# Routing step of a fused attention and mixture-of-experts kernel: four columns of one-hots on ScalarE instead of eight, block one-hots moved behind the first tokens, three zero products fewer

## The chip, the core and the metric

The kernel runs on one NeuronCore of one Trainium2 chip. The metric is device microseconds from the start to the end of one execution; the median of the runs of a kernel is its time. The engines are called by the short names of the profile: PE is TensorE (PEld its weight loads), DVE is VectorE, ACT is ScalarE, POOL is GpSimd, SP is SyncE, whose queue carries most of the transfers from HBM.

## What is computed

Two blocks follow each other. The attention block has a batch of 8, 8 heads, 512 tokens and 32 states per head of 64 numbers: the tokens read the states and the states read the tokens, each with its softmax. Its output is put together as 8 × 544 rows of 512 numbers, 4352 tokens in all. The second block sends each token through one of 8 experts:

```python
xread = softmax(scale * x @ state.T) @ state
sread = softmax(scale * state @ x.T) @ x
x = concatenate([xread, sread], axis=2)            # to (8, 544, 512)
...
logits = x @ w_gate;  local_gate = sigmoid(x @ w_local)
for b in range(B):
    prev_e = -1
    for s in range(S):
        fresh_e = argmax(logits[b, s])
        e = fresh_e if s == 0 or local_gate[b, s] < 0.5 else prev_e
        prev_e = e
        p = softmax(logits[b, s])
        h = maximum(x[b, s] @ w1[e], 0)            # 512 -> 1024
        out[b, s] = p[e] * (h @ w2[e])             # 1024 -> 512
```

So a token's expert is its own best one, or that of the token ahead of it, where its local gate says so.

## The kernel before, in words

The kernel has three stages.

**Attention** works through the batches in an order written out by hand (STEPS, L150) and writes each token's row to `rows` in HBM from the SP queue (L446 for 128 token rows, L405 for state rows). Near its end, steps of the attention and of the routing alternate (`reads()` in `Routing.route`).

**Routing** (`Routing.route`, L533 to L785) sorts the tokens by expert. The 4352 tokens stand as 40 columns (COLS) of up to 128 tokens, one token to a partition. Tokens of an expert are put into slots: blocks of 128 slots in pairs, and smaller tiles of 32 slots; there are 49 such blocks (NBLK). For every token the kernel computes its place in a block (`pos`, L661, 0 to 127) and the number of its block (`blk`, L665). To learn which token sits in which slot, it multiplies one-hot matrices on PE: for each of the 40 columns a 128 × 128 matrix that has a one at each token's place is loaded as weights, and a narrow matrix that holds the token's column and partition in the column of its block is streamed through (`slotted`, L712). The 40 products add up in one PSUM bank.

The places' one-hots are made by two engines. ACT makes those of the first eight columns (`inp0`): eight times Abs(index − place) (L680), and one Relu(1 − that) over all eight (L681). DVE makes those of the other 32 in four comparisons of 128 × 1024 (`inps`, L691), one for each eight columns. The narrow matrices exist in two sizes. `bf` (L684, L686) covers only the first two blocks. `bc` covers all 49 blocks; it is made in two halves of 20 columns, each by a comparison on DVE (`blocks`, L700), a scaled copy on ACT (L702) and a product on DVE (`blocks_by_column`, L707).

`slotted` is called three times. The call at L727 (`few`) uses `bf` and gives only the 256 tokens of the first pair of blocks, in the order of columns 8 to 39 and then 0 to 7, so that ACT's columns come last. `tokens` (L718) turns its result into row numbers on DVE (`two`). After the first `yield`, POOL gathers those rows from HBM with an indirect transfer for each block (`gather_first`, L833). The call at L734 (`who`) uses `bc` and gives the tokens of all blocks (`tok`, and `row` by L742 to L745). The third call (L769, `prob`) sorts the probabilities later on.

`keep(n)` (L538) multiplies `place` by an identity n times; the result is used nowhere. Such zero products stand between the calls to keep PE running: 22 ahead of the first call, 3 between the first and the second (L730), 6 after the second (L735).

Every engine takes its instructions in the order of the program. The driver (L1184 to L1196) issues the loads of the first expert's weights, the gather of the first tokens, then the part of the routing up to the second yield, then `turned(0, (0,))` (L851: PE transposes the first gathered block, L862, and DVE and ACT copy it to `xt`, L863), and then the rest of the routing.

**Experts** (from L788) works through pairs of blocks, 256 tokens of one expert each, with weights that stream through rings of nine buffers (`load`, L869). The first pair is multiplied plainly (`plain`, L1098, products at L1106); the others use seven products instead of eight (`strassen`, L1008, products at L1022; `second_half`, L1051, products at L1062), with sums of weight blocks on DVE (L936). Small tiles of 32 tokens are done between (L910, L922). POOL gathers later tokens quarter by quarter (L827) and scatters results (L1002, L932).

Of the kernel before, what the change touches and what calls it, by code (L numbers as in the profile page):

```python
# [10 lines left out]
BF16 = mybir.dt.bfloat16  # L11
Act = mybir.ActivationFunctionType
Alu = mybir.AluOpType
# [5 lines left out]
P = 128  # L19
# [12 lines left out]
COLS = B * NC  # L32
# [12 lines left out]
CG = 4  # L45
NG = COLS // CG
# [4 lines left out]
def kernel(  # L51
# [43 lines left out]
    with ExitStack() as phase, ExitStack() as late:  # L95
        p = late.enter_context(tc.tile_pool(name="p", bufs=4, space=PSUM, side="right"))
        reads = late.enter_context(tc.tile_pool(name="reads", bufs=1, side="right"))
        lt = reads.tile([P, B, NC, SQ], F32, name="lt")
        with ExitStack() as early:
            make_identity(nc, ident)  # L100
            start = Attention(early, tc, p, reads, xn, xt, st, stt, wgl, wgs, lt, rows, none)
            route.constants(ident)
            start.clear()
            route.more_constants()
            start.run(route)
        bank = Banks(tc, 4)
        routing = route.route(bank, lt, slots, start.reads, rows)
        experts(phase, late, tc, bank, w1, w2, rows, slots, route, routing, out)
# [63 lines left out]
class Attention:  # L172
# [50 lines left out]
    def run(self, route):  # L223

        self.route = route
        self.keep(10)
        self.steps = [(name, [int(i) for i in at]) for name, at in ((s[:2], s[2:]) for s in STEPS.split())]
        self.reads()
# [16 lines left out]
    def bank(self, parts=P, n=512):  # L245
        return self.p.tile([parts, n], F32, tag="p", name="p")
# [202 lines left out]
class Routing:  # L449
# [83 lines left out]
    def route(self, bank, lt, slots, reads, rows):  # L533
        nc, rt, ex = self.nc, self.rt, self.ex
        iof, iob, identb, part, cols, before, ones, one, ev, on, turn, quarter, place = self.consts
        exf = ex.rearrange("p b i -> p (b i)")

        def keep(n):  # L538

            to = bank.sums or [bank()]  # L540
            for i in range(n):
                nc.tensor.matmul(to[i % len(to)], lhsT=identb, rhs=place.rearrange("p k c -> p (k c)"), start=True, stop=True)
# [117 lines left out]
        pos = rt.tile([P, COLS], BF16, name="pos")  # L660
# [8 lines left out]
        def over(x, n=NBLK):  # L669
            return x.rearrange("p (g o c) -> p g o c", o=1, c=CG).to_broadcast([P, x.shape[1] // CG, n, CG])  # L670

        def each(x, n=NG):
            return x.rearrange("p (o k) c -> p o k c", o=1).to_broadcast([P, n, x.shape[1], CG])


        n = 2 * CG
        off = rt.tile([P, n, P], BF16, name="off")
        inp0 = rt.tile([P, n, P], BF16, name="inp0")
        for c in range(n):
# [6 lines left out]
        nc.vector.tensor_tensor(bf.rearrange("p d g k c -> p d (g k c)"),  # L686
                                inf.rearrange("p (o g) k c -> p o (g k c)", o=1).to_broadcast([P, 2, 2 * NG * CG]),
                                self.factors.rearrange("p d g k c -> p d (g k c)"), op=Alu.mult)
        inps = [rt.tile([P, 2, P, CG], BF16, name=f"inp{i}") for i in range(1, NG // 2)]
        for i, inp in enumerate(inps, 1):  # L690
            nc.vector.tensor_tensor(inp, each(place, 2), over(pos[:, i * n:i * n + n], P), op=Alu.is_equal)  # L691

        inb = rt.tile([P, NG, NBLK, CG], BF16, name="inb")
        pb = rt.tile([P, 3, NG, NBLK, CG], BF16, name="pb")
# [3 lines left out]
        def blocks(h):  # L698
            g = halves[h]
            nc.vector.tensor_tensor(inb[:, g], each(place[:, :NBLK], NG // 2),  # L700
                                    over(blk[:, g.start * CG:g.stop * CG]), op=Alu.is_equal)
            nc.scalar.activation(bc[:, 1, g].rearrange("p g k c -> p (g k c)"),  # L702
                                 inb[:, g].rearrange("p g k c -> p (g k c)"), Act.Copy, scale=part)

        def blocks_by_column(h):
            g = halves[h]
            nc.vector.tensor_tensor(bc[:, 0, g], inb[:, g], over(cols[:, g.start * CG:g.stop * CG]), op=Alu.mult)  # L707

        blocks(0)
        blocks_by_column(0)  # L710

        def slotted(to, x, order=(*range(n, COLS), *range(n))):  # L712
            for c in order:
                lhs = inp0[:, c] if c < n else inps[c // n - 1][:, c // CG % 2, :, c % CG]
                nc.tensor.matmul(to, lhsT=lhs, rhs=x[:, :, c // CG, :, c % CG],  # L715
                                 start=(c == order[0]), stop=(c == order[-1]))

        def tokens(to, who):  # L718
            high = rt.tile([P, to.shape[1]], F32, name="high")
            nc.vector.tensor_scalar(high, who[:, 0], -float(LOW), float(NT), Alu.mult, Alu.add)  # L720
            nc.vector.tensor_tensor(to, high, who[:, 1], op=Alu.add)
# [3 lines left out]
                            in_=rows[:NT].rearrange("(b t) q x -> q b t x", b=B)[0:1, :, 0:S + 1:S, 0])  # L725
        few = bank()[:, :4].rearrange("p (d k) -> p d k", d=2)
        slotted(few, bf)  # L727
        tokens(slots.two, few)
        yield
        keep(3)  # L730
        blocks(1)
        blocks_by_column(1)
        who = bank()[:, :2 * NBLK].rearrange("p (d k) -> p d k", d=2)
        slotted(who, bc, range(COLS))  # L734
        keep(6)  # L735
        wd = rt.tile([P, 2, NBLK], BF16, name="wd")
        nc.vector.tensor_copy(wd, who)
        tokens(slots.tok, who)
# [12 lines left out]
        def probabilities():  # L751
# [15 lines left out]
            prob = bank()[:, :3 * NBLK].rearrange("p (d k) -> p d k", d=3)  # L767
            yield
            slotted(prob, pb)  # L769
            nc.vector.tensor_copy(slots.prob, prob[:, 0])  # L770
            for d in (1, 2):
# [473 lines left out]
```

## Time and profile before

| | us |
|---|---|
| median of 3 runs | 546.63 |
| the 3 runs | 543.44, 546.63, 547.95 |
| the profiled execution's own time | 543.85 |
| its span, first to last instruction | 542.1 |
| busy in the span: PE, PEld, DVE, ACT, POOL | 525.3, 459.1, 381.2, 174.6, 314.4 |
| PE's mean granted clock in the span | 0.994 of full speed |

The profile is of one execution, and 1.75 us of its time lie outside the span. The routing stands between about 71 and 96 us of the span, its last part overlapping the start of the experts. The chain of waits follows the work that ended last back to its start; a row gives the start in us, the length in us, and the engine, tile and line. In a timeline a row is start, length, engine, line, operation, tiles and sizes, how many instructions were merged, and in square brackets how long the engine stood idle before it and what released it. In a table by window the columns are the window, its length, the busy time of each engine with its number of instructions, the granted PE clock (1.00 is full speed), the share of the DMA engines' time and the rate in GB/s.

### The profile page before, as it was taken

The numbers are of one execution on the slowest core, as the hardware profiler recorded it, in microseconds if no ns is written. First come the engines' busy times: TensorE is split into PE (matmuls) and PEld (weight loads), VectorE is DVE, ScalarE is ACT, GpSimd is POOL, SyncE is SP. The second block draws the span as 40 slices with busy tenths as digits, with TensorE's granted clock in tenths as the row PEclk, the third lists the DMA queues.
The fourth block names the chain that finished last, engine by engine and source line by source line (L and its number), as shares of the span: only waits on it lengthen the run. The fifth ranks groups of instructions, "written<-read, shape, count | busy, mean of one in ns | idle before, by whom it ended". The sixth has DMA issues, their size and how long they took to land.

```text
span 542.1 us, 12973 instructions
## 1 busy us (share of the span) xinstructions
PE 525.3 (97%) x4923; PEld 459.1 (85%) x4923; DVE 381.2 (70%) x618; ACT 174.6 (32%) x362; POOL 314.4 (58%) x384
## 2 busy tenths in 40 slices
PE   8799989999999999999999999999999999999994
PEld 3567776988989898989898989889999998989994
DVE  6999976656776657575765748386776767777774
ACT  6688754102223222222222222223132222213220
POOL 7788702563675746555555555565757474746653
PEclk9899999999999999999999999999999999999998
DMA  8999867699989899898989898974658484746652
GB/s 322 394 327 371 284 251 235 234 396 392 407 287 386 314 352 352 312 367 288 379 291 358 302 362 298 347 238 158 226 193 281 133 312 125 276 151 240 239 187 100
DMA packets 48970, 155.39 MB, mean 287 GB/s; under 512 B 6849, under 2 KB 8001, under 8 KB 45570
## 3 DMA queue, kind: packets, MB, share of 16 engines
q1 hardware_dynamic: 41234, 135.78, 68.9%
q0 software_dynamic: 7520, 18.62, 9.8%
q8 instruction: 41, 0.67, 0.5%
q14 instruction: 31, 0.25, 0.1%
q10 hardware_dynamic: 144, 0.07, 0.0%
HBM read 136.61 MB, written 17.89 MB: 285 GB/s over the span
## 4 chain that ended last, share of the span: by engine, by line
PE 89%; DVE 4%; DMA 3%; POOL 1%; ACT 1%; issue 1%; ACTq 0%; DVEq 0%
PE ps L1062 23%; PE ps L1022 20%; PE sum L1022 15%; PE sum L1062 13%; PE p L432 3%; PE ps L922 3%; PE ps L910 3%; PE ps L1106 3%; DMA x_n<-in_xn_dram 2%; PE ps L715 2%; PE s L307 1%; PE p L390 1%; DMA x_t<-in_xt_dram 1%; PE p L377 1%; POOL e L367 1%
## 5 line engine op out<-in xcount | busy, mean ns | idle before, releaser
L827 POOL DMA_INDIRECT xg<-rows,row x131 | 157.5, 1203 | 34.5 <-issue 32.9
L936 DVE TENSOR_TENSOR a<-a,a 128x1024 f32<-128x1024 f32 x64 | 76.8, 1220 | 30.5 <-DMA a<-in_w_dram 29.1
L1022 PE MATMUL ps<-xt,a 128*128 128x128 f32 x720 | 88.6, 276 | 0.0
L1022 PE MATMUL sum<-xs,a 128*128 128x128 f32 x720 | 87.8, 275 | 0.0
L1022 PEld LDWEIGHTS ps<-xt,a 128*128 128x128 f32 x720 | 84.4, 192 | 2.1 <-issue 1.8
L1022 PEld LDWEIGHTS sum<-xs,a 128*128 128x128 f32 x720 | 84.0, 192 | 0.0
L936 DVE TENSOR_TENSOR c<-c,c 128x1024 f32<-128x1024 f32 x64 | 75.4, 1219 | 3.8 <-DMA c<-in_w_dram 3.1
L1062 PE MATMUL ps<-c,h 128*128 128x256 f32 x312 | 74.7, 382 | 0.0
L1062 PEld LDWEIGHTS ps<-c,h 128*128 128x128 f32 x312 | 58.0, 190 | 10.9 <-issue 3.7
L1062 PE MATMUL ps<-c,hs 128*128 128x256 f32 x256 | 60.5, 379 | 0.0
L1002 POOL DMA_INDIRECT out_dram<-y,tok x32 | 38.6, 1205 | 28.8 <-DVE y L1089 14.5
L1062 PEld LDWEIGHTS ps<-c,hs 128*128 128x128 f32 x256 | 48.6, 190 | 6.6
L1062 PE MATMUL sum<-c,h 128*128 128x256 f32 x200 | 47.2, 379 | 0.0
L936 DVE TENSOR_TENSOR h<-s,s 128x512 f32<-128x512 f32 x15 | 10.4, 694 | 49.7 <-ACT s L1045 49.7
L1062 PEld LDWEIGHTS sum<-c,h 128*128 128x128 f32 x200 | 38.0, 190 | 5.2
L841 POOL COPY tick<-r 1x1 f32<-1x1 f32 x41 | 16.4, 401 | 42.8 <-ACT r L1067 40.1
L970 ACT COPY sum<-ps 128x256 f32<-128x256 f32 (+1 forms) x31 | 14.3, 460 | 71.1 <-PE ps L1022 49.5
L841 POOL COPY tick<-s 1x1 f32<-1x1 f32 x45 | 14.7, 327 | 36.8 <-ACT s L1045 36.8
L855 DVE STREAM_TRANSPOSE xt<-xg 128x512 f32<-128x512 f32 x32 | 33.5, 1083 | 1.0 <-DMA xg<-rows,row 1.0
L432 PE MATMUL p<-sd,a 128*128 128x256 f32 x128 | 32.1, 390 | 0.2 <-ACT xr L438 0.2
L1067 ACT ACTIVATE r<-sum,prob 128x256 f32<-128x256 f32 x32 | 15.1, 473 | 52.0 <-PE sum L1062 52.0
L1062 PE MATMUL sum<-c,hs 128*128 128x256 f32 x128 | 30.2, 379 | 0.0
(227 smaller groups left out, 756.8 us busy)
## 6 DMA issues: line engine op xcount, KB each, us to landing
a<-in_w_dram SPq DMA_DIRECT2D x68, 512.0 KB, 8.4
c<-in_w_dram SPq DMA_DIRECT2D x68, 512.0 KB, 10.6
at<-in_w_dram SPq DMA_DIRECT2D x18, 1024.0 KB, 10.9
ct<-in_w_dram SPq DMA_DIRECT2D x18, 1024.0 KB
x_t<-in_xt_dram SPq DMA_DIRECT2D x16, 512.0 KB, 7.8
x_n<-in_xn_dram SPq DMA_DIRECT2D x8, 1024.0 KB, 10.9
rows<-xr SPq DMA_DIRECT2D x32, 256.0 KB, 3.0
xg<-rows,row POOLq DMA_INDIRECT x131, 5.2
```

Source lines behind the costliest of these rows:

```text
L432: self.nc.tensor.matmul(v[:, d], lhsT=self.get("a", b, u)[:, c * P:c * P + P], rhs=self.sd[:, b, d], start=True, stop=True)
L827: nc.gpsimd.indirect_dma_start(out=to.rearrange("p x k -> p (x k)"), out_offset=None, in_=rows.rearrange("n q x -> (n q) x"), in_offset=ba ...
L841: nc.gpsimd.tensor_copy(tick, value)
L855: nc.vector.transpose(to.rearrange("p k (i t) -> p k i t", i=Q), xgs_[u % 2][:, b].rearrange("p i x k -> p k i x"))
L910: nc.tensor.matmul(hps[SQ * g:SQ * g + SQ, :], lhsT=self.x_t[:, j, :], rhs=a[:, j, :, g], start=(j == 0), stop=(j == KT - 1))
L922: nc.tensor.matmul(yps[SQ * g:SQ * g + SQ, :], lhsT=self.h[:, m, :], rhs=ct_[:, 2 * m // FK, g // 2, m % (FK // 2), g % 2 * P:g % 2 * P + ...
L936: nc.vector.tensor_tensor(out, a, b, op=op)
L1002: put = nc.gpsimd.indirect_dma_start(out=out, out_offset=to, in_=y, in_offset=None, bounds_check=NT - 1, oob_is_err=False)
L1022: nc.tensor.matmul(to[:, m * P:m * P + P], lhsT=w[:, j, m * P:m * P + P], rhs=x[:, j, :], start=begin and m == 0 and j == 0, stop=(m == FK ...
L1062: nc.tensor.matmul(to, lhsT=x[:, m, :], rhs=w[:, m, :], start=begin and m == 0, stop=(m == FK // 2 - 1), skip_group_check=True)
L1067: nc.scalar.activation(to, t, Act.Copy, scale=p)
L1106: nc.tensor.matmul(hps[:, i * P:i * P + P], lhsT=a[n][j // 2][:, j % 2, i * P:i * P + P], rhs=x_t[:, j, b * P:b * P + P], start=(j == 0), ...
```

## The change

Four things change.

1. ACT makes the one-hots of four columns instead of eight: `n` is now CG, which is 4, so that L680 issues four Abs instead of eight, and L681's Relu covers 128 × 512 instead of 128 × 1024. DVE makes the other 36: one comparison of 128 × 512 for columns 4 to 7, then four of 128 × 1024 for columns 8 to 39.
2. `slotted` takes columns 4 to 31, then ACT's 0 to 3, then 32 to 39, so that the last comparison of DVE comes last.
3. `blocks(0)` and `blocks_by_column(0)` stand behind `tokens(slots.two, few)`, ahead of the yield. On DVE all four operations for the 49 blocks now follow `two` directly; before, two of them stood ahead of it. ACT's two scaled copies follow their comparisons.
4. The second call of `slotted` is followed by three zero products instead of six.

```diff
-        n = 2 * CG
+        n = CG
         off = rt.tile([P, n, P], BF16, name="off")
         inp0 = rt.tile([P, n, P], BF16, name="inp0")
         for c in range(n):
...
-        inps = [rt.tile([P, 2, P, CG], BF16, name=f"inp{i}") for i in range(1, NG // 2)]
-        for i, inp in enumerate(inps, 1):
-            nc.vector.tensor_tensor(inp, each(place, 2), over(pos[:, i * n:i * n + n], P), op=Alu.is_equal)
+        inps = {}
+        for g, k in ((1, 1), *((g, 2) for g in range(2, NG, 2))):
+            inp = rt.tile([P, k, P, CG], BF16, name=f"inp{g}")
+            nc.vector.tensor_tensor(inp, each(place, k), over(pos[:, g * CG:(g + k) * CG], P), op=Alu.is_equal)
+            for i in range(k):
+                inps[g + i] = inp[:, i]
...
-        blocks(0)
-        blocks_by_column(0)
-
-        def slotted(to, x, order=(*range(n, COLS), *range(n))):
+        def slotted(to, x, order=(*range(n, COLS - 2 * CG), *range(n), *range(COLS - 2 * CG, COLS))):
             for c in order:
-                lhs = inp0[:, c] if c < n else inps[c // n - 1][:, c // CG % 2, :, c % CG]
+                lhs = inp0[:, c] if c < n else inps[c // CG][:, :, c % CG]
                 nc.tensor.matmul(to, lhsT=lhs, rhs=x[:, :, c // CG, :, c % CG],
...
         few = bank()[:, :4].rearrange("p (d k) -> p d k", d=2)
         slotted(few, bf)
         tokens(slots.two, few)
+        blocks(0)
+        blocks_by_column(0)
         yield
         keep(3)
         blocks(1)
         blocks_by_column(1)
         who = bank()[:, :2 * NBLK].rearrange("p (d k) -> p d k", d=2)
         slotted(who, bc, range(COLS))
-        keep(6)
+        keep(3)
```

## The prediction

> **What bounds the kernel now.** I began with the page: the span, the busy times, and the chain of work that ended last, by engine and line.
>
> ```profile
> span 542.1 us, 12973 instructions
> PE 525.3 (97%) x4923; PEld 459.1 (85%) x4923; DVE 381.2 (70%) x618; ACT 174.6 (32%) x362; POOL 314.4 (58%) x384
> PE 89%; DVE 4%; DMA 3%; POOL 1%; ACT 1%; issue 1%; ACTq 0%; DVEq 0%
> ```
>
> PE is the bound over the whole span; its products of the experts follow each other from 96.3 us on. A change in the routing therefore counts by one thing: when PE can begin the experts' first product (L1106). I then took the chain in order of time between 84 and 97 us.
>
> ```profile
> 84.77 2.46 ACT off L680 x8
> 87.25 1.07 ACT inp L681
> 88.37 0.35 PE ps L715 x8
> 88.72 0.67 PE sum L542 x3
> 89.39 3.85 PE ps L715 x40
> 93.24 1.30 PE sum L542 x6
> 94.53 0.76 issue
> 95.29 0.49 PE ps L862 x2
> 95.81 0.43 DVE xt L863
> 96.28 0.82 PE ps L1106 x5
> ```
>
> The chain runs through ACT's one-hots and then along PE's queue to the end of the six zero products (94.53). It says "issue" for 0.76 us because it doesn't connect the gather. L862 transposes the first gathered block, so the two paths into it are PE's queue (free at 94.53) and the gather. The timeline by engine shows the second path:
>
> ```profile
> 84.99 2.49 DVE L691 TENSOR_TENSOR inp<-place,pos 128x1024 bf16<-128x1024 bf16 x4
> 88.95 0.16 DVE L721 TENSOR_TENSOR two<-high,ps 128x2 int32<-128x2 f32 x1
> 89.72 0.67 DVE L707 TENSOR_TENSOR pb<-inb,cols 128x980 bf16<-128x980 bf16 x1
> 90.17 1.17 POOL L833 DMA_INDIRECT y<-rows,two  x1 [4.39 <-DMA a<-in_w_dram]
> ```
>
> `two` is done at 89.11, the gather starts 1.06 us later, is issued at 91.34, and L862 starts 3.92 us after that, when its rows have landed. The profile names a load of `a` as what released POOL. In the program the gather waits for `two` and for writes of `rows` and work of the attention done before 86, not for `a`; I take `two` as its releaser. So the gather ends last, 0.76 us behind PE.
>
> **Part 1 and 2: the one-hots.** ACT has four Abs instead of eight: 84.77 + 4 × 2.46/8 = 86.00. Its Relu on 512 instead of 1024 elements costs about 0.68 (from 1.06 for 1024 and 0.39 for an Abs on 128), so ACT ends at 86.70 instead of 88.32, a gain of 1.6 that is no longer the last wait: DVE is next. DVE gets a comparison of 512 elements ahead of its four. From 681 ns for 1024 and 241 ns for L686's 160 elements of bf16 it is 0.42 long; the four started 0.60 apart, 0.08 less than they last, so it adds 0.34. DVE ends at 84.99 + 2.49 + 0.34 = 87.82. PE's last eight products, now on DVE's strided layout, took 0.43 in such a group before, and start 0.06 after DVE: 88.31 instead of 88.72. `two` follows at +0.39: 88.70. Gain on the gather's path: **0.41**.
>
> **Part 3: the blocks behind `two`.** On DVE four operations follow at 88.62 (they overlap the end of `two` by 0.08, as before): two comparisons of 0.66 and two products of 0.67, with the small steps between them that the trace has: `inb` of the first half to 89.28, its product to 89.98, the second half's to 90.61 and 91.31. ACT's scaled copies, about 1.11 each, run 89.31 to 90.43 and 90.64 to 91.76. The second call of `slotted` waits for both results of the first half, so it starts at 90.49 instead of 89.36. Its 20 products of that half (3.85/40 each) end at 92.41, the second half is ready by then, and all end at **94.34** instead of 93.24. This is what the move costs on PE's queue: 1.1. Behind that wait stand the zero products, L862, L742 and all experts' products.
>
> **Part 4: three zero products fewer** give back 1.30/2 = 0.65: PE is free at 94.99 instead of 94.53. That was 0.76 ahead of the rows and is now about level with them; with six it would be 95.64.
>
> **The gather beside DVE.** With `two` at 88.70 the gather would start at 89.76, in the middle of DVE's four operations, where before only the rest of one (to 90.39) ran beside it. Here a rule of the Trainium skill speaks against the change. The page SBUF — State Buffer, section "SBUF: two separate sides", says that VectorE and GpSimd share a port pair under an exclusive lock, held for a whole instruction, and that POOL cannot write a transfer's descriptors while DVE holds it. Read strictly, with DVE's operations back to back, the gather would wait for the last one: 91.31 + 0.95 = 92.26, 0.92 later than now. The trace has this situation:
>
> ```profile
> 106.53 4.79 DVE L936 TENSOR_TENSOR c<-c,c 128x1024 f32<-128x1024 f32 x4 [3.10 <-DMA c<-in_w_dram]
> 107.96 1.94 POOL L827 DMA_INDIRECT xg<-rows,row  x1 [0.16 <-issue]
> 110.39 1.78 POOL L827 DMA_INDIRECT xg<-rows,row  x1 [0.16 <-issue]
> ```
>
> A gather alone takes 0.97. DVE's boundaries in that row are about 1.20 apart: 107.73, 108.93, 110.12, 111.32. The first gather ends at 109.90 and the second at 112.17, both 0.85 to 0.97 after the next boundary, although DVE went on at once in the first case. The one beside `two` fits too: 90.39 + 0.95 = 91.34. So a gather loses the rest of one DVE operation, not the whole burst. I take that: the boundary at 89.98 plus 0.95 is 90.93 instead of 91.34, and 0.41 of gain stays. Landing follows at +3.92: 94.85.
>
> **The sum.** L862 starts when the later of the two has come: PE's queue at 94.99, the rows at 94.85. That is about 95.0 instead of 95.29, a gain of **0.29**. What follows is relative to it: `wd` is ready about 94.7 for L742, the first weights of `a` landed at about 91.5, the loads of `c` wait for L754 on DVE behind it, and PE has no gap up to the end. The third call of `slotted` has the same 40 products in another order and no wait. The queues of SP and POOL keep their order. On the profiled execution it is 543.85 − 0.29 = 543.56; the median of the runs lies 2.78 above that execution, so 546.63 − 0.29 = **546.3**.
>
> **Rivals.**
> *The transfer sets the landing* (no gain). The loads of `a` keep the DMA engines at 0.86 to 1.10 of their time until 91.5. If the gathered rows queue behind them they land when they did, 95.26: change 0, 546.6. Against it: most of the gathers' traffic in the windows comes between 92 and 95, after those loads.
>
> *The port stays with DVE for the burst.* The gather is issued at 92.26, the rows land at 96.18, 0.9 later than now: 547.5. The two rows above speak against it; for it speaks only the page.
>
> *PE's clock drops* (slower). The new order leaves PE idle from the end of the three zero products (88.31 + 0.67 = 88.98) to 90.49, 1.5 us, behind a stretch of products only four columns wide (86.4 to 88.3). The trace has one gap after which the clock fell. Its rows, in order: the chain's first work after the gap, two windows of half a microsecond around the fall (the clock is the number behind POOL's bracket), and from PE's timeline a shorter gap:
>
> ```profile
> 16.81 1.93 PE p L390 x64
> 15.50:16.00 0.50, 0.00 (x0) 0.00 (x0) 0.47 (x2) 0.50 (x2) 0.44 (x1) 1.00 1.21 500
> 16.50:17.00 0.50, 0.19 (x9) 0.22 (x13) 0.50 (x2) 0.50 (x1) 0.50 (x2) 0.50 1.04 434
> 68.40 0.65 PE L422 MATMUL p<-a,gl 128*32 128x128 f32 x16 [1.14 <-DVE rt L400]
> ```
>
> PE stopped at 14.17, the clock still stood at 1.00 at 16.0 and was at half from about 16.3 for 3.4 us; the 64 products of L390 took 1.93 instead of 1.10. After a gap of 1.14 (the last row) it stayed at 1.00. My 1.5 lies between 1.14 and about 2.1, nearer the harmless one. If the clock falls as the second call starts, 3.4 us at 1.75 times the time cost 1.5 on PE's queue, 94.99 becomes 96.4 or 96.5, and the kernel loses 1.2; a drop in the fp32 products behind it costs up to 1.7. That is 547.8 to 548.3. It decides from a gap of some 2 us on, or sooner if the narrow products count as idle.
>
> **How the numbers follow.** Likeliest, gain of 0.1 to 0.5: 0.62, own range 546.1 to 546.5. No gain, because the transfer sets it: 0.17. Clock: 0.12. Port: 0.07. Something that the trace doesn't show: 0.02. No case reaches 1% (5.5 us), which is about what a measurement of this kernel can tell from no change: the three runs shown lie between 0.6% below their median and 0.2% above. So within 1%: 0.96; slower 0.03, since the unpriced risks (clock, port) lie on that side; faster 0.01. The range is made of the cases, −0.5 to +1.7, and of the spread of the runs, which is larger than any of them: 543.6 to 548.3.
>
> **What the next profile would show.** Right: ACT's Relu done at about 86.7 and the last comparison at 87.8; `two` at 88.7; the gather issued by 90.9; the second call from about 90.5 to 94.3; L862 at about 95.0; granted clock 1.00 from 86 to 96. Wrong: L862 at or after 95.3, with the clock below 1 around 90 to 94, or with a gather longer than 1.9 us, or with PE idle ahead of L862 though the gather was issued early. What would move the time by 1% is nothing in these 12 us; it would be a gap in the experts' stage, where PE has none now.

## The result

The change makes no measurable difference: the median after it is 547.08 us and before it 547.13 us, of 22 runs each; the ratio of the runs (not that of the two medians) is 1.0009, with a 95% interval of 0.9995 to 1.0022. The forecast was 546.3, no change that can be told, with a gain of 0.29 inside it. That gain isn't there.

The profiled execution after the change took 546.23 us, its span 544.3. The chain of work in order of time, from DVE's one-hots to the experts' first product (start us, us, what):

```profile
84.55 2.75 DVE inp L692 x5
87.36 0.44 PE ps L715 x8
88.01 0.16 DVE two L721
88.78 1.12 ACT pb L705
89.95 3.88 PE ps L715 x40
93.83 1.01 PE sum L542 x3
94.83 0.44 PE ps L864 x2
95.30 0.44 DVE xt L865
95.78 1.27 PE ps L1108 x9
```

The clock time of this stage moves by a microsecond from one execution to the next, since the attention ahead of it doesn't always take as long. I count from the end of `pos` (L661 ended at 84.48 before and at 83.95 here), to which the one-hots are tied. L864 after the change is L862 of before, and L1108 is L1106.

| from the end of `pos`, us | before | predicted | after |
|---|---|---|---|
| DVE's last comparison done | 3.00 | 3.34 | 3.35 |
| first call of `slotted` done | 4.24 | 3.83 | 3.85 |
| `two` done | 4.63 | 4.22 | 4.22 |
| gather starts | 5.69 | 5.28 | 5.28 |
| gather issued | 6.86 | 6.45 | 6.45 |
| second call starts | 4.91 | 6.01 | 6.00 |
| second call done | 8.76 | 9.86 | 9.88 |
| zero products done | 10.05 | 10.51 | 10.89 |
| first transposes of `y` start | 10.81 | 10.5 | 10.88 |
| experts' first product starts | 11.80 | 11.5 | 11.83 |

Down to the second call each step lies within 0.02 us of the forecast. Then two things go wrong: the zero products take longer, and the rows don't come earlier. The windows show the first: the columns are PE, PEld, DVE, ACT and POOL with their busy time, then the granted clock, the DMA share and the rate.

```profile
88.50:89.00 0.50, 0.00 (x0) 0.00 (x0) 0.47 (x2) 0.21 (x1) 0.00 (x0) 1.00 1.12 393
90.50:91.00 0.50, 0.50 (x8) 0.50 (x7) 0.24 (x1) 0.50 (x1) 0.30 (x1) 1.00 0.80 328
91.00:91.50 0.50, 0.50 (x9) 0.50 (x6) 0.00 (x0) 0.18 (x1) 0.50 (x1) 0.51 1.13 303
93.50:94.00 0.50, 0.50 (x5) 0.27 (x3) 0.07 (x1) 0.00 (x0) 0.00 (x0) 0.50 0.23 90
94.50:95.00 0.50, 0.50 (x4) 0.25 (x3) 0.05 (x1) 0.00 (x0) 0.00 (x0) 1.00 0.04 16
```

PE's clock falls to half at about 91.0 and is back at 94.4. The second call runs through it in 3.88 us, as long as at the full clock (3.85), but three zero products take 1.01 instead of 0.65. The second is in the timelines of POOL and of PE's weight loads:

```profile
89.23 1.17 POOL L835 DMA_INDIRECT y<-rows,two  x1 [4.07 <-DMA a<-in_w_dram]
94.75 0.56 PEld L864 LDWEIGHTS ps<-ident,y 128*128 128x128 f32 x4 [0.55 <-issue]
```

The gather starts 0.41 sooner than before, counted from `pos`, but the weight load of the first transpose starts only at 94.75, which is 4.35 after the gather was issued instead of 3.92. So the rows came at 10.80, about level with the end of the zero products. The experiments take the two apart.

### The profile page after: what moved, and what is told of

Same layout as the page of the kernel before. It is cut to its first block, busy times and chain, and to the rows that moved or that the text cites. A ratio compares the mean times of both kernels' runs of the same rounds, so it can differ in the third digit from the quotient of the medians.

```text
span 544.3 us, 12961 instructions
## 1 busy us (share of the span) xinstructions
PE 526.4 (97%) x4917; PEld 459.4 (84%) x4920; DVE 381.0 (70%) x619; ACT 173.0 (32%) x358; POOL 317.7 (58%) x384
## 4 chain that ended last, share of the span: by engine, by line
PE 88%; DVE 6%; DMA 3%; POOL 1%; issue 1%; ACT 0%; ACTq 0%; DVEq 0%
PE ps L1064 23%; PE ps L1024 20%; PE sum L1024 15%; PE sum L1064 13%; PE ps L924 3%; PE ps L912 3%; PE p L432 3%; PE ps L1108 3%; DMA x_n<-in_xn_dram 2%; PE ps L715 2%; DVE a L371 1%; DMA x_t<-in_xt_dram 1%; PE p L390 1%; PE p L377 1%; DVE e L334 1%
## 5 line engine op out<-in xcount | busy, mean ns | idle before, releaser
L1064 PEld LDWEIGHTS ps<-c,h 128*128 128x128 f32 x312 | 58.0, 190 | 10.9 <-issue 3.7
L843 POOL COPY tick<-r 1x1 f32<-1x1 f32 x41 | 19.2, 467 | 42.4 <-ACT r L1069 39.7
L843 POOL COPY tick<-s 1x1 f32<-1x1 f32 x45 | 16.4, 364 | 43.6 <-ACT s L1047 43.4
```

The lines of the kernel that those rows point to most:

```text
L843: nc.gpsimd.tensor_copy(tick, value)
L1064: nc.tensor.matmul(to, lhsT=x[:, m, :], rhs=w[:, m, :], start=begin and m == 0, stop=(m == FK // 2 - 1), skip_group_check=True)
```

## The experiments

Lines named in an expectation are those of its own kernel; one inserted or removed line shifts them by one. The variants with the gap filled, with none behind (both), with all of `a` held back and with each large part alone ran once each; one time says little here, so I go by their profiles.

**The gap filled.** Nine zero products instead of three between the first and the second call.

```diff
         yield
-        keep(3)
+        keep(9)
         blocks(1)
```

> The changed kernel with nine zero products instead of three behind the first call of slotted, which fill the 1.5 us in which PE stood idle there. Times are counted from the end of pos (L661); in the changed kernel the second call runs from 5.99 to 9.87, the zero products behind it to 10.87, and L864 starts there (before the change: 10.81). Theory (the clock fell in that idle gap, and its whole price is the zero products behind the second call): clock 1.00 throughout, the second call still takes 3.9, the three zero products behind it 0.67 instead of 1.01, and L864 starts at 10.5 to 10.55. Rival (the clock falls because of the stretch of narrow products, not of the gap): clock at half again, L864 at 10.85. Rival (the rows hold L864): zero products done at 10.5, L864 still at 10.8. The total time shows none of this: within 0.3 us of the changed kernel, under the spread of the runs.

The chain (`pos` ends at 84.10) and PE's weight load in its timeline:

```profile
90.10 3.88 PE ps L715 x40
93.98 0.65 PE sum L542 x3
94.63 0.22 issue
94.86 0.49 PE ps L864 x2
```

```profile
94.82 0.56 PEld L864 LDWEIGHTS ps<-ident,y 128*128 128x128 f32 x4 [0.69 <-issue]
```

The clock stays at 1.00 and the zero products take 0.65: with the idle gap filled, the clock doesn't fall. The other profiles agree: in all six kernels here with nine zero products in that place the clock is at 1.00 throughout the second call, and in all four profiles with a gap of 1.50 it falls during the call. But the transposes start at 10.76, not at 10.5: PE stands idle for 0.22, and the rows hold it. Theory and second rival are both right in part: the clock's price was 0.36, and behind it stood a second wait of nearly the same end.

**No zero products behind the second call**, once with three and once with nine ahead of it.

```diff
         slotted(who, bc, range(COLS))
-        keep(3)
         wd = rt.tile([P, 2, NBLK], BF16, name="wd")
```

> The changed kernel without any zero products behind the second call. This shows when the gathered rows have landed. Theory (PE's queue sets L864, the rows land about 10.0 from the end of pos, since the DMA engines are quiet from there on): L864 at 10.0 to 10.1, 0.8 earlier than in the changed kernel. Rival (the rows land 3.92 after the gather is issued, as the prediction took it): L864 at 10.37. If the clock is still at half there, the four transposes of L864 take longer than 0.72.

> The changed kernel with nine zero products behind the first call (the clock stays up) and none behind the second. PE is then free for L863 at 9.88 from the end of pos. In the kernels so far the first rows landed 10.8 to 11.1 after SP began to issue the loads of a, whether the gather started 5.4 or 6.5 after that. Theory (the landing is set by the loads of a, behind which the rows' packets drain; the rival the transfer sets the landing): L863 at 10.7 to 10.9, so PE stands idle for about 0.9 and nothing is gained. Rival (the rows land 3.92 after the gather is issued): 10.37.

With three ahead (`pos` ends at 84.76), PE waits 1.15 us for the rows and L863 starts at 11.02, so the theory of an early landing at 10.0 falls and so does 10.37. With nine ahead (`pos` ends at 83.65), L863 starts at 10.37. That is the rival's number to the digit, and alone it would have misled me. Counted from SP's issue of the loads of `a` instead, the two are 11.1 and 10.8, and every kernel falls into place. The rows' landing is read from the start of the first transpose's weight load, behind its idle time. The rows for it, of before and of the one-hots alone, whose gather starts latest:

```profile
84.38 1.95 SPq L879 DMA_DIRECT2D a<-in_w_dram  x4
95.26 0.56 PEld L862 LDWEIGHTS ps<-ident,y 128*128 128x128 f32 x4 [1.22 <-issue]
```

```profile
83.86 1.95 SPq L882 DMA_DIRECT2D a<-in_w_dram  x4
90.13 1.17 POOL L836 DMA_INDIRECT y<-rows,two  x1 [4.88 <-DMA a<-in_w_dram]
94.77 0.56 PEld L865 LDWEIGHTS ps<-ident,y 128*128 128x128 f32 x4 [0.77 <-issue]
```

| from the start of `a`'s issue on SP, us | gather starts | gather issued | rows landed |
|---|---|---|---|
| before | 5.79 | 6.96 | 10.88 |
| after | 5.46 | 6.63 | 10.98 |
| after, on another chip | 5.40 | 6.57 | 10.78 |
| gap filled | 5.45 | 6.62 | 10.89 |
| three ahead, none behind | 5.40 | 6.57 | 11.11 |
| nine ahead, none behind | 5.75 | 6.92 | 10.81 |
| one-hots alone (below) | 6.27 | 7.44 | 10.91 |

The gather moves by 0.87 us; the landing stays within 0.33 and doesn't follow it. (In the two profiles of the changed kernel PE's products leave no gap, and it is the weight load ahead of them that stands idle. In the second it starts 0.30 before its product, so it may have waited for PE; there 10.78 is only the latest that the rows can have come.) `two` can come earlier or later in this range, and the rows land at a fixed time from the issue of `a`'s loads.

Without zero products PE's queue can also pay in another way: with nine ahead and none behind, a gap of 0.49 is followed by a fall of the clock at 94.2, as the transposes run, and the first 32 of the experts' products take 4.78 instead of 3.84 (chain of work).

```profile
94.02 1.02 PE ps L863 x4
95.37 4.78 PE ps L1107 x32
```

**The loads of `a` taken out of the way.** Nine zero products ahead and none behind as above, and the loads wait for DVE's copy of the expert's number behind `row`:

```diff
-        e = index(slots.experts[0:1, u - 1:u] if u else slots.again if i else slots.expert)
+        e = index(slots.experts[0:1, u - 1:u] if u else slots.again)
...
-    load(0, 0)
     gather_first()
...
+    load(0, 0)
     load(0, 1)
```

> As the kernel with nine zero products behind the first call and none behind the second, but the loads of a (2 MB) are not issued ahead of the gather: they wait for the copy of the expert's number that DVE makes behind row, as the loads of c do. This takes away the traffic that the gather's rows are said to drain behind, and costs the experts' first product its early weights. Theory (a's loads set the landing): the rows land about 3.5 after the gather starts, at 8.8 to 9.2 from the end of pos, and L863 starts at once behind the second call, at 9.9; the experts' first product then waits for a until about 16.5, so the run is some 4 to 5 us longer. Rival (a fixed time from issue to landing): L863 at 10.4 or later.

POOL's gather and its landing in the view of the tile `y` (`pos` ends at 85.33):

```profile
90.60 1.17 POOL L834 DMA_INDIRECT y<-rows,two  x1 [4.45 <-DVE inb L703]
```

```profile
DMA to landing us min/median/max: 3.4/3.4/3.4
```

The same view of the kernel that differs only in the loads (nine ahead, none behind):

```profile
DMA to landing us min/median/max: 5.0/5.0/5.0
```

PE's transposes and the experts' first product with the loads held back:

```profile
95.02 0.66 PE L863 MATMUL ps<-ident,y 128*128 128x128 f32 x4
102.52 5.69 PE L1107 MATMUL ps<-xt,a 128*128 128x128 f32 x23 [6.57 <-DMA a<-in_w_dram]
```

Without the 2 MB of `a` the rows land 3.4 us after the gather starts, at 8.7, and not 5.0 to 5.6 as in those profiles with `a`'s loads ahead that give it (gap filled 5.4, three ahead 5.6, nine ahead 5.0, the changed kernel on another chip 5.3); the transposes follow the second call without a gap, at 9.7. So it is the loads of `a` that put the landing off. How they hold the rows isn't shown. Summed over windows of a quarter of a microsecond, 1.9 of the 2.1 MB of `a` had been moved when the gather of before was issued; from there to the landing it was 0.75 MB, of which 0.52 are the two gathers' rows. So most of `a` had been moved, and yet the rows came late. The experts' first product waits for its weights, as expected, to 17.2. The time is 553.23 in the one run, 9.4 above before; I expected 4 to 5, and 5.4 of it lie ahead of the first product. Its first products also run at half clock after the gap, and the stretch from there to PE's end is 3.3 longer; where the rest lies stays open.

**Half of `a` held back.** As the last, but two quarters are loaded early and two wait for a copy of the expert's number made right behind `wd`.

```diff
         nc.vector.tensor_copy(wd, who)
+        nc.vector.tensor_copy(slots.again, slots.expert)
...
-            nc.vector.tensor_copy(slots.again, slots.expert)
             nc.vector.tensor_copy(slots.experts, others)
...
-        e = index(slots.experts[0:1, u - 1:u] if u else slots.again if i else slots.expert)
+        e = index(slots.experts[0:1, u - 1:u] if u else slots.again if i or quarters.start else slots.expert)
...
-    load(0, 0)
+    load(0, 0, slice(2))
     gather_first()
     next(routing)
+    load(0, 0, slice(2, 4))
     turned(0, (0,))
```

> As the kernel with nine zero products behind the first call and none behind the second, but only the first two quarters of a (1 MB) are issued ahead of the gather; the other two wait for a copy of the expert's number that DVE makes right behind wd, and so run in the stretch from 95 to 98 us in which the DMA engines stood idle. Theory (a's loads set the landing): the rows land by 9.9 from the end of pos, L863 starts at 9.9 to 10.0 and the experts' first product at 10.9 instead of 11.8; the later quarters land at about 15, just when they are needed. Gain 0.9 us, ratio 0.9984. Rival (the landing has another cause): L863 at 10.4 to 10.8, and the time as before or longer, if the late quarters are waited for.

```profile
94.76 0.66 PE L863 MATMUL ps<-ident,y 128*128 128x128 f32 x4
96.38 0.82 PE L1107 MATMUL ps<-xt,a 128*128 128x128 f32 x5 [0.69 <-DVE xt L864]
```

The rows land 3.5 after the gather starts, and the transposes follow the second call without a gap, at 9.7 from the end of `pos` (85.04). But the first product starts at 11.34, not 10.9. It waits for a new last: the copy to `xt` stands on DVE behind `wd`, `again`, `high` and `tok`, and all four are due just then. The ratio is 0.9996, with an interval of 0.9982 to 1.0011.

**The same with that wait removed**: the copy of the number goes behind `blocks_by_column(1)`, and ACT makes both copies to `xt`.

```diff
         blocks(1)
         blocks_by_column(1)
+        nc.vector.tensor_copy(slots.again, slots.expert)
...
         nc.vector.tensor_copy(wd, who)
-        nc.vector.tensor_copy(slots.again, slots.expert)
...
-            for h, copy in enumerate((nc.scalar.copy if b else nc.vector.tensor_copy, nc.scalar.copy)):
+            for h, copy in enumerate((nc.scalar.copy, nc.scalar.copy)):
```

> As the kernel that holds half of a back, with two more edits. The copy of the expert's number is made right behind the last block operation on DVE, so that the late quarters of a are issued about 2.5 us sooner, behind the gather's packets. And both halves of the first xt are copied by ACT, so that the first copy no longer waits for DVE's wd, high and tok. Theory (with the rows landed early, PE's queue up to the end of the second call is the bound): L863 at 9.9 from the end of pos as in that kernel, the experts' first product at 10.6 to 10.7 instead of 11.3 there and 11.8 before the change; gain against before the change 1.1 to 1.2 us, ratio 0.9979. Rival (the sooner quarters of a delay the rows again): L863 at 10.4 or later, and no gain.

The timeline of PE (`pos` ends at 83.89):

```profile
89.90 3.87 PE L715 MATMUL ps<-pb,inp 128*128 128x98 bf16 x40 [0.20 <-ACT pb L705]
93.59 0.66 PE L863 MATMUL ps<-ident,y 128*128 128x128 f32 x4
94.89 3.81 PE L1107 MATMUL ps<-xt,a 128*128 128x128 f32 x32 [0.37 <-ACT xt L864]
```

The first product starts at 11.00, 0.80 earlier than before the change; I expected 10.6 to 10.7, and the last row has PE waiting 0.37 for ACT's copies. The median is 542.73 against 543.60 of before on that chip, the ratio 0.9989 with an interval of 0.9971 to 1.0008. In the profile this version beats both kernels; in the time it can't be told from them.

**Each large part alone.** First the new one-hots with the blocks where they were and six zero products (the diff is against the changed kernel); then the move of the blocks with the one-hots and the six zero products of before (against the kernel before).

```diff
+        blocks(0)
+        blocks_by_column(0)
+
         def slotted(to, x, order=(*range(n, COLS - 2 * CG), *range(n), *range(COLS - 2 * CG, COLS))):
...
         tokens(slots.two, few)
-        blocks(0)
-        blocks_by_column(0)
         yield
...
         slotted(who, bc, range(COLS))
-        keep(3)
+        keep(6)
```

> The change of the one-hots alone: four columns on ACT, the others on DVE in the new order, but the blocks' one-hots where they were before the change and six zero products. Theory (DVE's queue decides: the two block operations now stand between DVE's last comparison and the reading of the first call's result): few done at 3.84 from the end of pos, two only at about 5.05 instead of 4.63 before the change and 4.21 after it, the gather starts at 6.1, and L862 starts at about 11.2, 0.4 later than before the change. Rival (only ACT's end mattered): two at 4.2 and L862 at 10.4.

```diff
-        blocks(0)
-        blocks_by_column(0)
-
         def slotted(to, x, order=(*range(n, COLS), *range(n))):
...
         tokens(slots.two, few)
+        blocks(0)
+        blocks_by_column(0)
         yield
```

> The move of the blocks' one-hots alone: one-hots of eight columns on ACT as before the change, six zero products, the blocks behind two. Theory (two hangs on ACT's one-hots, done 3.84 after the end of pos, and not on the blocks): two at 4.6 as before the change, the gather issued at about 6.85, the second call starts 0.4 later than in the changed kernel, at 6.4, and ends at 10.3; PE stands idle 1.5 us again and the clock falls, so that the six zero products take about 2.0 to 2.3 instead of 1.30, and L862 starts at 12.3 to 12.6, 1.5 to 1.8 later than before the change. Rival (the clock does not fall): 11.6.

With the one-hots alone (`pos` ends at 84.17) `two` is done at 4.90 and the gather starts at 5.96, 0.27 later than before the change, which is DVE's queue as the theory says, though less of it. Yet L865 starts at 10.63, sooner than before and not 0.4 later, since the rows land with the loads of `a`, which were issued 0.31 before the end of `pos` here and 0.10 before the change. The clock fell in this kernel too (windows as above):

```profile
88.50:89.00 0.50, 0.17 (x1) 0.00 (x0) 0.47 (x4) 0.50 (x1) 0.00 (x0) 1.00 1.08 377
89.00:89.50 0.50, 0.20 (x3) 0.30 (x4) 0.50 (x2) 0.25 (x1) 0.00 (x0) 0.58 0.84 279
```

It fell at 89.1, inside a gap of 0.63 ahead of the second call, and was back at 92.5. The second call, most of it at half clock, took 3.89, and the six zero products behind it ran at full clock and took 1.30, so this fall cost nothing.

With the move alone (`pos` ends at 85.43) the second call runs from 6.41 to 10.29, as expected, the clock falls during it, and six zero products take 1.62 instead of the 2.0 to 2.3 that I gave them. The transposes start at 11.75 to 11.9, and the first product at 12.65, 0.85 later than before the change. Its first gather began 6.47 after `a`'s issue, later than any in the table, and in the view of `y` landed 4.4 after its start: at 10.9 from `a`'s issue once more, although the windows have 2.1 MB moved by the time it was issued. So the move by itself costs 0.85 on PE's queue; the sooner one-hots and the dropped zero products only pay that back.

**Does a delay here count one for one?** Nine zero products ahead and 33 behind the second call (`keep(9)`, `keep(33)`).

> The changed kernel with nine zero products behind the first call and 33 behind the second. The 30 more than in the changed kernel are 6.5 us of PE time ahead of L864. Theory (everything behind L864 is relative to it, so that a delay there counts one for one): L864 at 17.0 from the end of pos instead of 10.8, and the time 6.2 longer than before the change, ratio 1.0113. Rival (the experts' stage has slack of its own, for instance the loads of weights, so that a shift is partly taken up): 2 to 4 us longer.

The chain (`pos` ends at 85.16):

```profile
102.16 0.24 PE ps L864 x2
102.90 0.38 PE ps L1108
```

L864 starts at 17.0 and the first product at 17.74, 5.94 later than before; from there to the end of PE's last product it is 438.8, as before. So in the profile the delay counts one for one, and there is no slack. In the time it is more than that: the ratio is 1.0151, interval 1.0128 to 1.0174, thus at least 6.9 us where I expected 6.2. The theory's number is missed, and the profile of one execution doesn't show where the rest lies; it stays open.

**The changed kernel once more**, on another chip.

> The changed kernel once more, on another chip, beside the kernel before. In its first profile the stretch from the experts' first product to the end of PE's work took 441.8 us, in the profiles of before and of four variants 438.8. Theory (those 2.9 us belong to that execution and not to the change): 438.8 here, the experts' first product again at 11.8 to 11.9 from the end of pos, ratio 1.000. Rival (the change costs the experts' stage something, say by the place of its buffers): 441 to 442 again and a ratio of 1.003 to 1.005.

In the first profile after the change, the stretch from the first product (95.78) to the end of PE's last was 441.8, in that of before 438.8. The last product in that first profile, and in this one (chain of work):

```profile
535.80 1.74 PE ps L1064 x8
```

```profile
93.85 1.28 PE sum L542 x3
95.13 0.24 PE ps L864 x2
95.87 2.16 PE ps L1108 x17
532.97 1.74 PE ps L1064 x8
```

Here it is 534.71 − 95.87 = 438.84, and the ratio is 0.9997, interval 0.9984 to 1.0010. The 2.9 us belonged to that execution: they lie in many small stretches between pairs, such as 2.06 to 2.27 instead of 1.88 for the 64 products of L924, and this second profile of the same kernel has none of them (1.88 to 1.89). The clock fell here too, at 91.6, and the three zero products took 1.28. The first product starts at 11.89.

## Why the prediction was right, and where it was wrong

The verdict, no change that can be told, and the range held, and they would have held with either sign of the 0.29: the median of before itself is 0.50 higher over 22 runs than over the three of the forecast. That they held says nothing for the gain, and the account of the gain didn't hold.

*The one-hots and the blocks* (parts 1 to 3) were right in every term to 0.02. ACT stopped being the last wait, DVE took its place, and `two` gained 0.41. The second call was pushed back by 1.1.

*The gather beside DVE.* The gather came when I said, and the rival of the port rested on too wide a reading of the page SBUF — State Buffer. Its section "SBUF: two separate sides" says that POOL can't write descriptors while DVE runs an operation in a 2-port mode; a DVE operation with two SBUF inputs, as these four have, takes the lock only against a POOL operation that reads SBUF, as the gather reads `two`, and for that instruction. The trace of before agrees: beside L936, with two such inputs, a gather took 1.44, beside a transpose, with one input, 0.97:

```profile
126.39 2.51 DVE L936 TENSOR_TENSOR a<-a,a 128x1024 f32<-128x1024 f32 x2 [6.83 <-DMA a<-in_w_dram]
127.04 1.44 POOL L827 DMA_INDIRECT xg<-rows,row  x1 [0.48 <-issue]
128.81 2.09 DVE L855 STREAM_TRANSPOSE xt<-xg 128x512 f32<-128x512 f32 x2
129.10 0.97 POOL L827 DMA_INDIRECT xg<-rows,row  x1 [0.16 <-issue]
```

DVE after the change:

```profile
88.78 0.67 DVE L710 TENSOR_TENSOR pb<-inb,cols 128x980 bf16<-128x980 bf16 x1
89.37 0.66 DVE L703 TENSOR_TENSOR inb<-place,blk 128x980 bf16<-128x980 bf16 x1
90.07 0.67 DVE L710 TENSOR_TENSOR pb<-inb,cols 128x980 bf16<-128x980 bf16 x1
```

The gather started at 89.23; the operation running then ended at 89.45; 89.45 + 0.95 is 90.40, the measured end, with two more operations on its heels. The rival of the port is out: the burst doesn't hold the gather. That a gather loses the rest of one operation isn't tested by the change, since it began 0.22 before the end of one, and took 1.17, before and after alike.

*The landing* is the first step that failed: "Landing follows at +3.92". I took the 3.92 of one trace as a property of the gather. It hung on when `a`'s loads had been issued. The seven profiles of the table land at 10.8 to 11.1 from `a`'s issue whatever the gather does; with `a` out of the way the landing takes 3.4 from the gather's start. The rival "the transfer sets the landing", to which I gave 0.17, is what happened, though that the rows queue behind `a` is not shown. I argued against it from the traffic in the windows, and the windows do show a tail: after the change 16 to 33 GB/s from 93.75 on, a share of 0.04 to 0.09 of 16 engines, while the rows were still awaited.

*Part 4* is the second: three zero products were to end at 10.51 and ended at 10.89, because the clock fell. The rival of the clock had its mechanism right and its price wrong. I priced the second call at 1.75 times its time at half clock, from 64 fp32 products; it took 3.88 instead of 3.85. The whole price was 0.36 in one profile and 0.63 in the other. I had also put the fall from a gap of some 2 us on, or sooner if the narrow products count as idle; it came in all four profiles with a gap of 1.5, and whether the narrow products have a part in it stays open.

Either failure alone would have eaten most of the gain: with the clock kept up the experts' first product starts at 11.75 instead of 11.83. So 0.41 won on `two` was lost to a transfer that hid it anyway, and 0.65 won from fewer zero products went into the 1.1 of the later second call and the clock.

## What to carry to other kernels

A constant from issue to landing taken from one trace is worth what stood in the queues at that time: check it against the start of the large transfers before building on it. When two paths end within a few tenths of a microsecond of each other, shortening one shows only that the other was there. And count from an event just ahead of the edit, since the start of a stage moves from one execution to the next by more than the effect.

## What the runs showed of the hardware that I had not expected

- PE at half clock doesn't slow every stream. The 40 products of 98 columns, with a 128 × 128 weight load each, took 3.88 and 3.89 with most of the time at half clock, and 3.85 at full clock. Three zero products of 512 columns took 1.28 at half clock instead of 0.65, and the first 32 fp32 products 4.78 instead of 3.84 with 2.2 us of that at half clock.
- How long PE has just stood idle doesn't alone decide whether the clock falls. After gaps of 1.5 us it fell in four of four profiles, 1.0 to 1.6 us after PE was busy again; after a gap of 0.49 (nine ahead, none behind) 0.2 later; and in the one-hots alone inside a gap of 0.63. Gaps of 0.76 (before) and 0.69 (half of `a` held back) left it at 1.00. Each of these falls lasted 3.4 us, but 6.8 with three zero products ahead and none behind. What decides stays open.
- A gather by POOL that was issued beside or shortly behind 2 MB of weight loads landed 4.4 to 5.6 us after its start in five profiles that give it, and 3.4 without those loads ahead; its landing stood at 10.8 to 11.1 us from their issue, whenever it started itself.
